# VectorE's order in a key phase, the load of the key weights, and the split of a routed update, in a linear-attention kernel with a routed MLP

## The chip, the core and the metric

The kernel runs on one core of one Trainium2 chip. The metric is the device time of one execution in microseconds; times before are the median of three runs. A profile is one further execution, taken by the hardware profiler; its span runs from the first to the last instruction.

The engines: PE (TensorE: matmuls and transposes through the array), PEld (the weight loads of PE), DVE (VectorE), ACT (ScalarE), POOL (GpSimd) and SP (SyncE, which here only issues DMAs). Each engine executes its own instructions in the order of the program and waits at semaphores for others.

## The reference

```
xn = layernorm(x)                              # x: 2048 x 640, no scale or bias
q, k, v = split(xn @ wqkv)                     # 32 heads of 20
phi = lambda t: where(t > 0, t + 1, exp(t)) + 1e-6
kv = einsum("bhsd,bhde", phi(k), v);  z = sum_s phi(k)
A  = ((phi(q) @ kv) / (phi(q) . z + 1e-6)) @ wo
r  = xn @ w_r                                  # a score of each row
idx = the 8 rows with the largest r
y  = ((silu(xn[idx] @ w_gate) * (xn[idx] @ w_up)) @ w_down) * sigmoid(r[idx])
B  = xn, with y added to the rows idx
out = x + A + B
```

All tensors are bfloat16.

## The kernel before

The 2048 rows are 16 tiles of 128 rows (t = 0 to 15), the 640 columns 5 blocks of 128 (kc). Tensors that stay in SBUF: `XX[:, t, 0, :]` holds the normalised tile and `XX[:, t, 1, :]` the input tile; `xnT` the normalised rows transposed; `pk` phi(k); `pqT` phi(q), transposed; `wk` the key weights. The values are never computed: `Gs`, the product of the normalised rows with phi(k), is multiplied by the value weights instead. All engines' instructions stand in an order written out by hand.

**Start (to about 19 us).** SP loads tiles 0, 1 and 2, then the key weights in two halves of 320 columns (`wkh[0]`, L112, and `wkh[1]`, L131), then tile 3 and the others. The second half lies in SBUF in rows of 321: its last column holds the router's vector `w_r`, which PE transposes into PSUM bank 3 (L128) and ACT copies (L130). Warm-up matmuls on zeros (L117, by `warm`) run on PE meanwhile. The first tiles are transposed by PE (`tr_pe`), tiles from 4 on by DMA transposes that SP issues (`tr_dma`, L205).

**The layer norm of a tile**, with the names of the program: `ln_a` and `ln_b` are the statistics of the left and the right half of the row on DVE (L148, L151), `ln_g` aggregates them (L154), `ln_s` adds epsilon on DVE (t of L173) and takes the square root as a power on POOL (s of L175), `ln_c` forms the centred tile c on ACT (L180) or DVE (L182), and `ln_xn` takes the reciprocal (L187) and scales c into `XX` (L189), both on DVE. For tiles 1 and 5 ACT makes the statistics (`ln_act`, `ln_var`).

**The k phase (about 19 to 54 us), a loop over t = 4 to 15 at L420.** `K(t)` is ten matmuls of the transposed tile by the key weights (L227, two halves into PSUM banks 6 and 7; the second half has the router's column too). `PHa(t)` takes Exp and Relu of both halves on ACT (L243, L246), `PHb(t)` forms phi(k) from them on DVE, min(exp, 1) + relu (L262, called the feature sum here), and `G(t)` accumulates nine matmuls into PSUM (L267, L272). PE's order is K(t), G(t-1). DVE's order in an iteration is: feature sum of t-1; reciprocal and scaling of tile t+2; both half statistics, the aggregate and t of tile t+3. ACT's is: four activations of tile t, then c of tile t+3. SP issues the transpose of tile t+2, and from t = 7 on a part of the query weights behind it; at t = 13 it issues the loads of the other weights (wv, wo, wg, wu).

**Residual.** x + xn is formed in place in `XX[:, t, 1, :]` (`xpx`): on DVE (L214) for tiles from `TF` on, at the end of the k phase, and on ACT (L217) for tiles below `TF`, during the output phase.

**The later phases (PE without a break from 47.6 us).** `q_pe` and `q_fin` make phi(q) in 20 blocks (L453, L508); between them stand the small products for kv, z and the routed MLP. From 87.5 us on `out_one(t)` multiplies by the merged output weights (L684), adds the residual on DVE (L698, for the last tile in two halves, L694) and stores the tile (SP; the second half of the last tile goes through ACT's queue).

**The routed update** is y for 8 rows. `TF` splits it: the residual tiles from TF on are written to a scratch in HBM (`hi_copy`), y is added there by an accumulating indirect DMA of POOL (`hi_add`, in `rows_add`, L712), and they are loaded back (`hi_load`) before their output tiles need them. For tiles below TF the outputs are stored first, and y is then added to the output in HBM by a second accumulating DMA (`fix_add`, the same line), which stands in front of the last output tile and waits for the stores of all tiles below TF. Rows outside of the half in question have an index out of bounds and are skipped.

Of the kernel before, what the change touches and what calls it, by code (L numbers as in the profile page):

```python
# [7 lines left out]
P = 128  # L8
S = 2048
D = 640  # L10
# [3 lines left out]
T = S // P  # L14
KC = D // P
# [7 lines left out]
FQ = F // 4  # L23
EPS_BF16 = 1.0013580322265625e-05
LOW = S - 1
TF = 12

BF16 = mybir.dt.bfloat16
F32 = mybir.dt.float32
# [7 lines left out]
def kernel(  # L37
# [13 lines left out]
    pe, dve, act, pool, sp = nc.tensor, nc.vector, nc.scalar, nc.gpsimd, nc.sync  # L51
# [3 lines left out]
    wqkv_v = A_wqkv.rearrange("(kc p) n -> p kc n", p=P)  # L55
# [7 lines left out]
    PS = psp.tile([P, 8, 512], F32, name="PS")  # L63

    def st(shape, dt, name, tag=None):
        return sb.tile(shape, dt, name=name, tag=tag or name)
# [2 lines left out]
    xnT = st([P, KC, S], BF16, "xnT")  # L69
    pk = st([P, T, D], BF16, "pk", "pkwd")  # L70
    pqT = st([P, KC, S], BF16, "pqT")
    wk = st([P, KC * (D + 1)], BF16, "wk", "wkM")
    wq = st([P, KC, D], BF16, "wq")
    wo1 = st([P, NG, D], BF16, "wo1")
    wo2 = st([P, D], BF16, "wo2")
# [5 lines left out]
    ident = st([P, P], BF16, "ident")  # L81
# [12 lines left out]
    MR = st([P, T], F32, "MR")  # L94

    HW = 320
    wkh = [wk[:, 0 : KC * HW].rearrange("p (k c) -> p k c", k=KC),
           wk[:, KC * HW : KC * (D + 1)].rearrange("p (k c) -> p k c", k=KC)]


    def ld(eng, dst, src):
        eng.dma_start(dst, src)
# [5 lines left out]
    wr = st([KC, P], BF16, "wr")  # L108
    ld(act, wr[:], B_w_r.rearrange("(kc p) -> kc p", p=P))
    ld(sp, XX[:, 1, 1, :], x_v[:, 1, :])  # L110
    ld(sp, XX[:, 2, 1, :], x_v[:, 2, :])
    ld(sp, wkh[0], wqkv_v[:, :, D : D + HW])  # L112


    def warm(n, w=512):
        for _ in range(n):
            pe.matmul(PS[:, 7, 0:w], lhsT=zero[:, 0:P], rhs=zero[:, 0:w], start=True, stop=True)  # L117
# [7 lines left out]
    dve.memset(ones32[:], 1.0)  # L125
    dve.memset(eps6[:], 1e-6)
    warm(4)
    pe.transpose(PS[:, 3, :].bitcast(BF16)[:, 0:KC], wr[:], ident[0:KC, 0:KC])  # L128
    warm(6)
    act.copy(wkh[1][:, :, HW], PS[:, 3, :].bitcast(BF16)[:, 0:KC])  # L130
    ld(sp, wkh[1][:, :, 0:HW], wqkv_v[:, :, D + HW : 2 * D])  # L131
    ld(sp, XX[:, 3, 1, :], x_v[:, 3, :])
    kv1 = st([P, NG, GC], BF16, "kv1")
    kv2 = st([P, NG, GC], BF16, "kv2")
# [11 lines left out]
    def ln_a(t):  # L146
        sts[t] = tmp.tile([P, 2, nc.vector.BN_STATS_DIM], F32, tag="stats", name="stats", bufs=3)
        dve.bn_stats(out=sts[t][:, 0, :], in_=XX[:, t, 1, 0:320])  # L148

    def ln_b(t):  # L150
        dve.bn_stats(out=sts[t][:, 1, :], in_=XX[:, t, 1, 320:D])  # L151

    def ln_g(t):
        dve.bn_aggr(out=MV[:, t, :], in_=sts[t][:])  # L154
# [15 lines left out]
    def ln_s(t, sg=1.0):  # L170
        t2 = tmp.tile([P, 1], BF16, tag="t2", name="t2", bufs=4)
        ss[t] = tmp.tile([P, 1], BF16, tag="s", name="s", bufs=4)
        dve.tensor_scalar(out=t2[:], in0=MV[:, t, 1:2], scalar1=sg, scalar2=EPS_BF16,  # L173
                          op0=ALU.mult, op1=ALU.add)
        pool.tensor_tensor(out=ss[t][:], in0=t2[:], in1=halfc[:], op=ALU.pow)  # L175

    def ln_c(t, eng):
        cs[t] = tmp.tile([P, D], BF16, tag="c", name="c", bufs=3)
        if eng is act:
            act.activation(cs[t][:], XX[:, t, 1, :], AF.Identity, bias=MVf[:, t, 0:1], scale=-1.0)  # L180
        else:
            dve.tensor_scalar(out=cs[t][:], in0=XX[:, t, 1, :], scalar1=MVf[:, t, 0:1], scalar2=-1.0,  # L182
                              op0=ALU.subtract, op1=ALU.mult)

    def ln_xn(t, parts=((0, D),)):
        c = cs[t]
        dve.reciprocal(SR[:, t : t + 1], ss[t][:])  # L187
        for a, b in parts:
            dve.tensor_scalar(out=XX[:, t, 0, a:b], in0=c[:, a:b], scalar1=SR[:, t : t + 1], scalar2=-1.0,  # L189
                              op0=ALU.mult, op1=ALU.mult)  # L190
# [13 lines left out]
    def tr_dma(t):  # L204
        sp.dma_start_transpose(xnT[:, :, t * P : (t + 1) * P], XX[:, t, 0, :])  # L205
# [6 lines left out]
    def xpx(t):  # L212
        if t >= TF:
            dve.tensor_scalar(out=XX[:, t, 1, :], in0=XX[:, t, 1, :], scalar1=SR1[:, t : t + 1],  # L214
                              scalar2=MR[:, t : t + 1], op0=ALU.mult, op1=ALU.add)
            return
        act.activation(XX[:, t, 1, :], XX[:, t, 1, :], AF.Identity, bias=MR[:, t : t + 1], scale=SR1[:, t : t + 1])  # L217


    def off(t, h):  # L220
        return T - 1 - t if t != 1 and h else 0

    def K(t, hs=(0, 1), b=6):
        for h in hs:
            w = HW + h
            for kc in range(KC):
                pe.matmul(  # L227
                    PS[:, b + h, off(t, h) : off(t, h) + w],
                    lhsT=xnT[:, kc, t * P : (t + 1) * P],
                    rhs=wkh[h][:, kc, 0:w],  # L230
                    start=(kc == 0),
                    stop=(kc == KC - 1),
                )
# [6 lines left out]
    def PHe(t, h, b=6):  # L240
        if h == 0:
            phis[t] = tuple(tmp.tile([P, D], BF16, tag=k, name=k, bufs=3) for k in ("ek", "rk"))
        act.activation(phis[t][0][:, h * HW : (h + 1) * HW], phi_src(t, h, b), AF.Exp)  # L243

    def PHr(t, h, b=6):
        act.activation(phis[t][1][:, h * HW : (h + 1) * HW], phi_src(t, h, b), AF.Relu)  # L246

    def PHa(t, hs=(0, 1), b=6):
        for h in hs:
            PHe(t, h, b)  # L250
            PHr(t, h, b)
# [8 lines left out]
    def PHb(t):  # L260
        ek, rk = phis[t]
        dve.scalar_tensor_tensor(out=pk[:, t, :], in0=ek[:], scalar=1.0, in1=rk[:], op0=ALU.min, op1=ALU.add)  # L262
# [99 lines left out]
    ln_xn(1)  # L362
    ln_g(2)
    ln_s(2)
    K(0, (0,))
    PHe(0, 0)
    tr_pe(1, 2, act, act)
    consts_e()
    bm2_copies(sp, (1, 2))
    PHr(0, 0)  # L370
    K(0, (1,))
    ln_c(2, dve)
    ln_a(3)
    ln_xn(2)
    PHa(0, (1,))
    K(1, (0,), 4)
    tr_pe(2, 0, act, act)
    K(1, (1,), 4)
# [16 lines left out]
    ln_s(4)  # L395
    PHr(2, 0)
    ln_c(4, dve)
    ln_xn(4)
    tr_dma(4)
    bm2_copies(act, (3,))  # L400
# [8 lines left out]
    ln_s(5, -1.0)  # L409
    ln_c(5, dve)  # L410
    PHa(3)
    ln_a(6)
    ln_xn(5)
    tr_dma(5)
    ln_b(6)
    ln_g(6)
    ln_s(6)
    ln_c(6, act)
# [1 line left out]
    for t in range(4, T):  # L420
        K(t)
        PHb(t - 1)
        if t + 2 < T:
            ln_xn(t + 2)
            tr_dma(t + 2)
        PHa(t)
        if t + 3 < T:
            ln_a(t + 3)
            ln_b(t + 3)
            ln_g(t + 3)  # L430
            ln_s(t + 3)
            ln_c(t + 3, act)
        if t == 13:
            xpx_cols(TF, T)
            xpx(TF)
        if t > 13:
            for i in range(2 if t == 14 else 1):
                xpx(TF + 1 + 2 * (t - 14) + i)
        G(t - 1)
        if t - 1 in pool_extra:  # L440
            pool_extra[t - 1]()
        if t > 4:
            loads(t)
# [261 lines left out]
    idxh = st([P, 1], I32, "idxh")  # L705
    hi_d = drp.tile([S - TF * P, D], BF16, name="hi_d")
    hi_4 = hi_d[:].rearrange("s (j c) -> (s j) c", j=4)
    hi_v = hi_d[:].rearrange("(t p) d -> p t d", p=P)
    out_lo = out[0][0 : TF * P, :].rearrange("s (j c) -> (s j) c", j=4)

# [175 lines left out]
```

## Time and profile before

| | us |
|---|---|
| median of three runs | 115.87 (115.63 to 115.9) |
| the profiled execution | 115.39 |
| its span, first to last instruction | 113.7 |

| engine | busy us | share of the span |
|---|---|---|
| PE | 105.9 | 93% |
| PEld | 65.0 | 57% |
| DVE | 83.8 | 74% |
| ACT | 76.2 | 67% |
| POOL | 24.2 | 21% |

The mean granted clock of PE is 0.994. DMAs move 18.72 MB, at 165 GB/s over the span. In a timeline a row gives the start, the duration, the engine, the line, the operation with its tiles and shapes, and in brackets the idle time of the engine just before with what ended it. Neighbouring instructions of one engine overlap a little in these records, so the distance of two starts says more than a duration. In the view of windows a row gives a stretch, its length, the busy time (and number of instructions) of PE, PEld, DVE, ACT and POOL, the granted clock, the busy share of the DMA engines and GB/s. A row of waits gives total time, number and longest one. A row of DMA issues gives KB each and the median time from issue to landing, where it is known.

### The profile page before, as it was taken

How to read it: one execution, taken by the hardware profiler on the slowest of the kernel's cores; microseconds unless marked ns; L12 is line 12 of the kernel's file. 1: busy time of each engine (PE TensorE's matmuls, PEld its weight loads, DVE VectorE, ACT ScalarE, POOL GpSimd, SP SyncE). 2: the span in 40 equal slices, each digit the busy share in tenths (PEclk: the TensorE clock that was granted, in tenths of full speed). 3: DMA queues.
4: the chain of work that ended last, by engine and by line, in shares of the span. 5: the costliest groups of instructions: out<-in, count | busy, mean ns of one | idle time of the engine just before them, and what ended most of it. 6: DMA issues, size and time to landing. Idle time of an engine off the chain costs nothing.

```text
span 113.7 us, 2754 instructions
## 1 busy us (share of the span) xinstructions
PE 105.9 (93%) x999; PEld 65.0 (57%) x999; DVE 83.8 (74%) x209; ACT 76.2 (67%) x168; POOL 24.2 (21%) x48
## 2 busy tenths in 40 slices
PE   5989997999899999999999999999999999999970
PEld 1356654665555555566657565656565767777740
DVE  1888898867777777784586996466867898869760
ACT  4649993866777766665199379799979965980000
POOL 7345214236433333300000002200033000000050
PEclk9999999999999999999999999999999999999997
DMA  3899932302344664429999946950712143693342
GB/s 87 244 271 356 310 64 53 62 21 39 61 115 115 63 159 89 99 58 279 355 390 401 403 145 167 389 160 26 244 42 47 35 141 118 123 378 131 127 157 62
DMA packets 22984, 18.72 MB, mean 165 GB/s; under 512 B 11194, under 2 KB 21690, under 8 KB 22970
## 3 DMA queue, kind: packets, MB, share of 16 engines
q1 hardware_dynamic: 22352, 18.36, 54.2%
q10 hardware_dynamic: 330, 0.16, 0.5%
q8 instruction: 8, 0.13, 0.5%
q0 software_dynamic: 288, 0.01, 0.3%
q14 instruction: 6, 0.05, 0.2%
HBM read 12.98 MB, written 3.49 MB: 145 GB/s over the span
## 4 chain that ended last, share of the span: by engine, by line
PE 50%; DVE 8%; POOL 3%; DMA 2%; POOLq 2%; issue 1%; ACT 0%; DVEq 0%
PE PS L453 19%; PE PS L684 14%; PE PS L267 4%; POOL s L175 3%; PE PS L227 2%; DMA out_dram<-o 2%; POOLq L881 2%; PE PS L622 2%; PE PS L628 2%; PE PS L646 1%; DVE stats L151 1%; DVE stats L148 1%; DVE XX L189 1%; PE PS L516 1%; PE PS L286 1%
## 5 line engine op out<-in xcount | busy, mean ns | idle before, releaser
L227 PE MATMUL PS<-wk,xnT 128*128 128x320 bf16 (+1 forms) x160 | 24.6, 300 | 1.0 <-DMA xnT<-XX 0.7
L267 PE MATMUL PS<-pk,XX 128*128 128x512 bf16 x80 | 23.2, 378 | 1.8 <-DVE pk L262 1.5
L453 PE MATMUL PS<-xnT,wq 128*128 128x512 bf16 x100 | 23.1, 380 | 0.0
L684 PE MATMUL PS<-Mb,pqT 128*128 128x320 bf16 x160 | 22.1, 299 | 0.0
L227 PEld LDWEIGHTS <-xnT 128*128 128x128 bf16 x160 | 15.3, 98 | 8.5 <-DMA xnT<-XX 1.3
L175 POOL TENSOR_TENSOR s<-t,halfc 128x1 bf16<-128x1 bf16 x16 | 14.0, 878 | 28.0 <-DVE t L173 28.0
L684 PEld LDWEIGHTS <-pqT 128*128 128x128 bf16 x160 | 15.5, 97 | 6.4
L453 PEld LDWEIGHTS <-wq 128*128 128x128 bf16 x100 | 11.4, 118 | 8.6
L243 ACT ACTIVATE ek<-PS 128x320 bf16<-128x320 f32 x32 | 14.0, 438 | 3.4 <-PE PS L227 3.3
L508 DVE SCALAR_TENSOR_TENSOR pqT<-qe,qr 128x512 bf16<-128x512 bf16 x20 | 13.5, 683 | 3.7 <-ACT qr L460 3.7
L459 ACT ACTIVATE qe<-PS 128x512 bf16<-128x512 f32 x20 | 12.1, 607 | 5.5 <-PE PS L453 5.4
L698 DVE TENSOR_TENSOR o<-PS,XX 128x640 bf16<-128x640 f32 x15 | 12.3, 823 | 3.9 <-PE PS L684 3.3
L180 ACT ACTIVATE c<-XX,MVf 128x640 bf16<-128x640 bf16 x10 | 8.3, 828 | 9.3 <-DVE MVf L154 5.5
L246 ACT ACTIVATE rk<-PS 128x320 bf16<-128x320 f32 x32 | 14.2, 443 | 0.0
L272 PE MATMUL PS<-pk,XX 128*128 128x128 bf16 x64 | 14.0, 218 | 0.0
L262 DVE SCALAR_TENSOR_TENSOR pk<-ek,rk 128x640 bf16<-128x640 bf16 x16 | 13.0, 817 | 0.6 <-ACT rk L246 0.6
L267 PEld LDWEIGHTS <-XX 128*128 128x128 bf16 x80 | 7.7, 97 | 8.1
L460 ACT ACTIVATE qr<-PS 128x512 bf16<-128x512 f32 x20 | 12.1, 607 | 0.0
L217 ACT ACTIVATE XX<-XX,MR,SR 128x640 bf16<-128x640 bf16 x12 | 10.2, 913 | 1.4 <-DVE o L698 1.4
L272 PEld LDWEIGHTS <-XX 128*128 128x128 bf16 x64 | 6.2, 97 | 4.3 <-issue 3.8
L148 DVE BATCH_NORM_STATS2 stats<-XX 128x6 f32<-128x320 bf16 x14 | 6.8, 488 | 2.5 <-DMA XX<-in_A_x_dram 2.4
L189 DVE TENSOR_SCALAR XX<-c,SR 128x640 bf16<-128x640 bf16 (+2 forms) x17 | 6.5, 387 | 1.7 <-ACT rk L246 0.5
(117 smaller groups left out, 100.5 us busy)
## 6 DMA issues: line engine op xcount, KB each, us to landing
out_dram<-o SPq DMA_DIRECT2D x15, 160.0 KB, 1.9
XX<-in_A_x_dram SPq DMA_DIRECT2D x6, 320.0 KB, 6.4
wg<-in_B_w_gate_dram SPq DMA_DIRECT2D x5, 384.0 KB, 6.8
wu<-in_B_w_up_dram SPq DMA_DIRECT2D x5, 384.0 KB, 6.9
wd<-in_B_w_down_dram SPq DMA_DIRECT2D x1, 1920.0 KB, 9.0
wk<-in_A_wqkv_dram SPq DMA_DIRECT2D x2, 400.0 KB, 4.3
wq<-in_A_wqkv_dram SPq DMA_DIRECT2D x5, 160.0 KB, 2.4
wv<-in_A_wqkv_dram SPq DMA_DIRECT2D x1, 800.0 KB, 4.8
```

Of the source, the lines that this page charges most:

```text
L175: pool.tensor_tensor(out=ss[t][:], in0=t2[:], in1=halfc[:], op=ALU.pow)
L227: pe.matmul(PS[:, b + h, off(t, h) : off(t, h) + w], lhsT=xnT[:, kc, t * P : (t + 1) * P], rhs=wkh[h][:, kc, 0:w], start=(kc == 0), stop=( ...
L243: act.activation(phis[t][0][:, h * HW : (h + 1) * HW], phi_src(t, h, b), AF.Exp)
L246: act.activation(phis[t][1][:, h * HW : (h + 1) * HW], phi_src(t, h, b), AF.Relu)
L262: dve.scalar_tensor_tensor(out=pk[:, t, :], in0=ek[:], scalar=1.0, in1=rk[:], op0=ALU.min, op1=ALU.add)
L267: pe.matmul(PS[:, a, :], lhsT=lhsT, rhs=pk[:, t, 0:512], start=(t == 0), stop=(t == T - 1),)
L272: pe.matmul(PS[:, 5, a * P : (a + 1) * P], lhsT=lhsT, rhs=pk[:, t, 512:D], start=(t == 0 and a == 0), stop=(t == T - 1), skip_group_check= ...
L453: pe.matmul(PS[:, bank, :], lhsT=by5(wq[:, kc, :])[:, m, :], rhs=xnT[:, kc, tb * TBLK : (tb + 1) * TBLK], start=(kc == 0), stop=(kc == KC ...
L459: act.activation(e, PS[:, bank, :], AF.Exp)
L508: dve.scalar_tensor_tensor(out=pqT[:, m, tb * TBLK : (tb + 1) * TBLK], in0=e, scalar=1.0, in1=r, op0=ALU.min, op1=ALU.add,)
L684: pe.matmul(PS[:, b + h, 0:HW], lhsT=pqT[:, kc, t * P : (t + 1) * P], rhs=Mb[:, kc, h * HW : (h + 1) * HW], start=(kc == 0), stop=(kc == K ...
L698: dve.tensor_tensor(out=ot[:].rearrange("p (h c) -> p h c", h=2), in0=PS[:, b : b + 2, 0:HW], in1=XX[:, t, 1, :].rearrange("p (h c) -> p h ...
```

## The change

Three edits in one.

1. In the k phase the first half statistic of a tile (`ln_a`) moves. For t below 9 it stands between the feature sum and the reciprocal of the same iteration; from t = 8 on the first half of tile t+4 is taken at the end of the iteration, ahead of the next feature sum (at t = 8 both happen). Ahead of the loop, the halves of tile 6 stand in front of `ln_xn(4)` and `ln_xn(5)`.
2. The key weights come in one load of whole rows of 640 columns; in SBUF the rows are 641 long, and both halves of K read from them. The router's column waits in PSUM bank 5 (before: 3), and ACT copies it behind the copies of the first transposed tile instead of ahead of the second load. There is one warm-up matmul less.
3. `TF` goes from 12 to 11: tile 11 passes from the group below TF to the group that goes through the scratch, its residual from ACT to DVE.

```diff
-TF = 12
+TF = 11
...
-    wk = st([P, KC * (D + 1)], BF16, "wk", "wkM")
+    wk = st([P, KC, D + 1], BF16, "wk", "wkM")
...
-    wkh = [wk[:, 0 : KC * HW].rearrange("p (k c) -> p k c", k=KC),
-           wk[:, KC * HW : KC * (D + 1)].rearrange("p (k c) -> p k c", k=KC)]
...
-    ld(sp, wkh[0], wqkv_v[:, :, D : D + HW])
+    ld(sp, wk[:, :, 0:D], wqkv_v[:, :, D : 2 * D])
...
     warm(4)
-    pe.transpose(PS[:, 3, :].bitcast(BF16)[:, 0:KC], wr[:], ident[0:KC, 0:KC])
-    warm(6)
-    act.copy(wkh[1][:, :, HW], PS[:, 3, :].bitcast(BF16)[:, 0:KC])
-    ld(sp, wkh[1][:, :, 0:HW], wqkv_v[:, :, D + HW : 2 * D])
+    pe.transpose(PS[:, 5, :].bitcast(BF16)[:, 0:KC], wr[:], ident[0:KC, 0:KC])
+    warm(5)
     ld(sp, XX[:, 3, 1, :], x_v[:, 3, :])
...
-                    rhs=wkh[h][:, kc, 0:w],
+                    rhs=wk[:, kc, h * HW : h * HW + w],
...
     ln_s(2)
+    act.copy(wk[:, :, D], PS[:, 5, :].bitcast(BF16)[:, 0:KC])
     K(0, (0,))
...
     ln_c(4, dve)
+    ln_a(6)
     ln_xn(4)
...
     PHa(3)
-    ln_a(6)
+    ln_b(6)
     ln_xn(5)
     tr_dma(5)
-    ln_b(6)
     ln_g(6)
...
         PHb(t - 1)
+        if t + 3 < T and t < 9:
+            ln_a(t + 3)
         if t + 2 < T:
             ln_xn(t + 2)
             tr_dma(t + 2)
         PHa(t)
         if t + 3 < T:
-            ln_a(t + 3)
             ln_b(t + 3)
             ln_g(t + 3)
             ln_s(t + 3)
             ln_c(t + 3, act)
+        if t + 4 < T and t >= 8:
+            ln_a(t + 4)
...
-            for i in range(2 if t == 14 else 1):
+            for i in range(2):
                 xpx(TF + 1 + 2 * (t - 14) + i)
```

## The prediction

> **What bounds the kernel now.** I read the page first: TensorE (PE) is busy 93% of the span, and the chain that ended last is PE from 47.6 us to 104.5 us with next to no gaps. Before that, from 35.7 to 46.9 us, the chain is something else, a loop through VectorE (DVE) and GpSimd (POOL), so I went to the k phase (the loop over t, about 19 to 54 us) and cut it at the starts of K(4) to K(15) in the view of windows. Three of the twelve:
>
> ```profile
> 21.74:24.42 2.68, 2.68 (x21) 1.69 (x19) 1.72 (x6) 2.24 (x5) 1.49 (x4) 1.00 0.32 64
> 36.70:39.88 3.18, 2.96 (x21) 1.64 (x19) 2.56 (x9) 2.14 (x5) 1.06 (x1) 1.00 0.56 58
> 48.94:51.62 2.68, 2.68 (x21) 1.69 (x20) 2.11 (x5) 1.43 (x4) 0.00 (x0) 1.00 0.49 76
> ```
>
> The first number is the length, then busy time of PE, its weight loads, DVE, ACT and POOL. A tile needs 2.68 us of PE; the tiles in the middle take about 3.06 to 3.18. Over 2.68 the nine intervals from K(6) at 24.42 to K(15) at 51.62 have 0.30, 0.49, 0.39, 0.38, 0.50, 0.26, 0.38, 0.38 and 0.00: **3.08 us** that PE doesn't need. The timeline of DVE for one such tile shows why:
>
> ```profile
> 37.59 0.81 DVE L262 SCALAR_TENSOR_TENSOR pk<-ek,rk 128x640 bf16<-128x640 bf16 x1
> 38.85 0.16 DVE L187 RECIPROCAL SR<-s 128x1 f32<-128x1 bf16 x1 [0.44 <-POOL s L175]
> 39.12 0.39 DVE L189 TENSOR_SCALAR XX<-c,SR 128x640 bf16<-128x640 bf16 x1
> 39.42 0.49 DVE L148 BATCH_NORM_STATS2 stats<-XX 128x6 f32<-128x320 bf16 x1
> 39.82 0.48 DVE L151 BATCH_NORM_STATS2 stats<-XX 128x6 f32<-128x320 bf16 x1
> 40.33 0.21 DVE L154 BATCH_NORM_AGGREGATE MVf<-stats 128x2 bf16<-128x12 f32 x1
> 40.58 0.16 DVE L173 TENSOR_SCALAR t<-MVf 128x1 bf16<-128x1 bf16 x1
> 40.65 0.82 DVE L262 SCALAR_TENSOR_TENSOR pk<-ek,rk 128x640 bf16<-128x640 bf16 x1
> ```
>
> From feature sum (L262) to feature sum 3.06 us pass, and 0.44 of them DVE waits for POOL's square root s (L175), which needs this tile's t. G(t) waits for the feature sum (six waits, 1.5 us on PE's view of waits), and the rest of the loss follows from it. In the view of waits this is 4.9 us in 11 waits of L187.
>
> How long POOL's power takes depends on what DVE runs beside it:
>
> ```profile
> 37.76 1.06 POOL L175 TENSOR_TENSOR s<-t,halfc 128x1 bf16<-128x1 bf16 x1 [2.00 <-DVE t L173]
> 16.70 0.62 POOL L175 TENSOR_TENSOR s<-t,halfc 128x1 bf16<-128x1 bf16 x1 [2.49 <-DVE t L173]
> 16.83 0.48 DVE L148 BATCH_NORM_STATS2 stats<-XX 128x6 f32<-128x320 bf16 x1
> ```
>
> At 37.76 it ends (38.82) 0.42 after the feature sum's end (38.40). At 16.70 it ends (17.32) 0.40 after the c of L182, which ran 16.54 to 16.92, while a half statistic runs from 16.83 to 17.31. So POOL seems held by the DVE instruction in front of it, then needs about 0.42, and a half statistic beside it doesn't hold it.
>
> **The k order, t below 9.** The first half statistic of tile t+3 goes from behind L189 into the gap behind the feature sum. Counts don't change, only places. New period from the rows: feature sum to reciprocal 38.85-37.59 = 1.26 (still set by POOL; 0.74 of sum plus 0.40 of statistic fit under it, 0.12 are left as wait), to L189 0.27, to the second statistic 0.30, to the aggregate 0.51, to t 0.25, to the next sum 0.07: 2.66 against 3.06. The whole 0.40 goes, and the loop is a hair below PE's 2.68. Then PE sets the pace and no more can be gained. L189, and with it the transpose that SP issues behind it, stands as far behind the sum as now, since the reciprocal waits for POOL in either order; ACT's c (L180) waits for the aggregate, which comes 0.40 earlier.
>
> **The order from t = 9 on.** The first half of tile t+4 stands behind t, ahead of the feature sum, so POOL's power (0.18 behind t) runs beside a statistic. Period: 0.07+0.40+0.74+0.27+0.30+0.51+0.25 = 2.54 if the power is out of the way, 2.69 if the sum waits until the power has had its 0.42 (0.18+0.42 = 0.60 behind t instead of 0.47, rounded up). Either is about PE's pace. What is given back: iteration 8 carries two first halves, 0.40 once; POOL's constants around 23 us held L189 from 23.29 to 23.70 and will again; one transpose took 2.18 us to issue (at 36.47), where 1.20 is usual. The sum may start 2.37 us (when ACT has finished) to 3.18 us (when G needs it, 4.05 less 0.87) behind its tile's K start, so 0.8 us of lag costs nothing and only what is above it stalls PE. All of the lags together are about 1.2 to 1.7, so I give back 0.5. Bounds: 3.08 (nothing given back) and 1.3 (rival one). Value: **2.6 us**. What follows is PE-bound, and its loads (wv, wo, wg, wu) are issued behind the last transposes, so all of it moves forward too.
>
> **Before the loop.** The first half of tile 6 takes the 0.44 us gap ahead of reciprocal 4, its second half the gap ahead of reciprocal 5 (17.35), so sum 3 comes 0.40 earlier than 18.69. No gain by itself: K(4) waits until 19.06 for a transpose, 0.68 us after PE's last busy record:
>
> ```profile
> 19.06 1.54 PE L227 MATMUL PS<-wk,xnT 128*128 128x320 bf16 x10 [0.68 <-DMA xnT<-XX]
> ```
>
> **The k weights in one load.** Now two of 400 KB, and the second waits for ACT's copy of the router column, though the columns differ:
>
> ```profile
> SPq L102 <- ACT wk L130: 0.9, 1, 0.9
> wk<-in_A_wqkv_dram SPq DMA_DIRECT2D x1, 400.0 KB, 4.3
> wv<-in_A_wqkv_dram SPq DMA_DIRECT2D x1, 800.0 KB, 4.8
> ```
>
> The first half was issued at 2.19 and landed 4.3 later, 6.49; K(0) began at 7.02, when xnT came. The whole is of wv's shape, which landed in 4.8 with nothing ahead; at 2.19 up to 1.3 us of x tiles are ahead (480 KB at some 350 GB/s, the rate of 9.5 to 10 us). So it lands at 7.0 to 8.3. The copy now stands on ACT behind the load and waits for it the same way (0.2 us with its hand-over), K(0) behind the copy; on ACT the first Exp and the copies of tile 1 are queued behind it. PE shifts by 0 to 1.3 us there, middle 0.6. Of this, 0.84 (18.22, where G(2) has been issued, to 19.06) is covered by the wait for the transpose; past it up to 0.5 shows. Against it: SP no longer stands from 2.62 to 3.49, so the x tile of L148's wait at 8.73 (0.57 us) may come up to 0.57 earlier and with it the transpose of tile 4, worth at most 0.4. I take **0.0**, bounds 0.4 gained to 0.5 lost. One warm-up matmul less (0.43) leaves PE idle from about 5.54 to 5.78: nothing waits for it.
>
> **Eleven tiles by accumulating DMA.** ACT loses one L217 (0.91 us, late, where it has 8 us free after 101.8); DVE gains one L214 (0.44) at t = 15, where it has no statistics left: free. hi_copy and hi_load grow from 640 to 800 KB, some 0.5 us each at 355 GB/s; the POOL add behind hi_copy started at 84.30 and its result is fetched at 96.57, so nine us cover it, and SP's stores queued behind hi_load have seven o buffers. At the end POOL's add waits for the store of tile 10 instead of 11, issued 1.46 us earlier (104.23 against 105.69). But two waits end together there:
>
> ```profile
> L881 SPq EVENT_SEMAPHORE  x2: 17/1030/2042, 110.4 to 110.4; - x2
> L881 POOLq DRAIN  x1: 3344/3344/3344, 109.0 to 109.0; - x1
> ```
>
> POOL's drain ends at 112.34, SP's wait for the last store at 112.44. Without POOL's part the store still ends there. I take **0.1** (fewer packets beside it), bounds 0 and 0.3.
>
> **Sum.** 2.6 + 0.0 + 0.1 = 2.7 us, against the profiled execution's own 115.39 (span 113.7 and 1.7 around it): 112.7. That execution is 0.48 below the median of the runs, 115.87, so the forecast for the median is **113.2 us**; its own range from the bounds is 112.2 to 114.0.
>
> **The rivals.**
> One: the wait is only partly removed, because POOL's power now gets ahead of the feature sum and holds it, or the transposes, issued 5.06 us behind a K start and needed 8.04 behind it, land late. For: the power's start, 0.18 behind t, is ahead of the sum wherever a statistic or ACT delays the sum. Against: only 0.42 of its time seems its own. If the sum is held by 0.35 in each tile the period is 2.89, and of 3.08 some 1.3 remain: 114.5 us.
> The Trainium skill's page "SBUF — State Buffer", section "Who interferes with whom", says that a DVE instruction with two SBUF inputs and a GpSimd instruction that reads SBUF lock each other out, whichever is first, for the whole instruction. The 1.06 against 0.62 us here agrees; by that rule the 0.35 is sure from t = 9 on and the time would lie between the two.
> Two: no change. If a statistic holds POOL as the sum does, the power ends 0.42 behind it, and the reciprocal stands at 0.74+0.40+0.42 = 1.56 with 0.07 of hand-over: 3.0 again, 115.7 us. The record at 16.70 speaks against it.
> Three, slower: the clock. With one warm-up matmul less and 0.24 us idle before the first transposes, PE could stay at its half rate (a 128x512 warm-up takes 0.43 apart at first, 0.22 later) through the early K and G. PE work from 6 to 18 us is 11 us; at half rate for all of it, 11 - 0.84 - 2.7 = 7.5 lost, 123 us; it decides against the change once the half rate lasts over 3.5 us of such work. Against: 0.68 us of idle before K(4) left the pace of its ten matmuls (1.54 us) as it is in every later K.
> The page "TensorE: Matmul & The Clock Gate", Part 1 of the Trainium skill, has the clock change after a window of about 3.4 us, so one missed window would cost an estimated 1.7 us, no sign change.
>
> **Chances.** Forecast 0.62, partial 0.20, no change 0.08, slower 0.10 (the clock, or what I don't see). 0.3% (0.35 us) is about what a measurement of this kernel can tell from none. Faster 0.82, same 0.08, slower 0.10. The range, 112.2 to 115.2, takes in most of the partial case.
>
> **What would show it.** DVE's reciprocal waits fall from 0.44 to about 0.1, K starts lie 2.68 to 2.75 apart from K(6) on, and DVE's loop leaves the chain. K(4) stays at 18.6 to 19.5. The last two waits: POOL's drain ends about 1.4 before SP's. I am wrong if K starts still lie 3.0 apart, if the sum waits behind the power, or if K(0) starts after 8.5 and K(4) moves with it.

## The result, and the profile after

| | us |
|---|---|
| before, median of 4 runs beside it | 115.89 (115.63 to 116.25) |
| after, median of 4 runs | 112.82 (111.42 to 114.36) |
| after / before | 0.9642, interval 0.9575 to 0.9709 |
| the profiled execution of after | 113.53 |
| its span | 111.7 (before: 113.7) |

The changed kernel is faster. Its executions fall into two groups by the mean granted clock of PE, and the ratio is made from the two in which the clock was kept (111.42 and 112.11); it stands for 0.9642 * 115.89 = 111.7 us. The forecast was 113.2, with 112.2 as its low end: the direction is right, and the gain of those executions is larger than I allowed.

The profiled execution is one of the others, so it shows what the change gains and what it loses in one picture. First the three intervals between K starts that answer to those of before, in the view of windows (length, busy time of PE, its weight loads, DVE, ACT and POOL, clock, DMA share, GB/s):

```profile
22.48:25.22 2.74, 2.74 (x21) 1.65 (x20) 2.52 (x8) 2.15 (x5) 1.61 (x4) 1.00 0.56 63
36.10:39.55 3.45, 2.83 (x20) 1.63 (x19) 3.27 (x10) 3.03 (x6) 1.10 (x2) 1.00 1.01 79
47.56:50.23 2.67, 2.67 (x20) 1.68 (x19) 1.54 (x4) 1.43 (x4) 0.00 (x0) 1.00 0.75 171
```

In ten of the eleven intervals from K(4) at 19.81 to K(15) at 50.23 PE is now busy from end to end, 2.66 to 2.84 us each. One, in front of K(11), is 3.45 and holds a wait of 0.62. K(4) to K(15) takes 30.42, against 32.56 before. DVE's timeline shows the new order, with no idle time in front of the reciprocal (L183, before L187):

```profile
28.20 0.81 DVE L258 SCALAR_TENSOR_TENSOR pk<-ek,rk 128x640 bf16<-128x640 bf16 x1
28.93 0.49 DVE L144 BATCH_NORM_STATS2 stats<-XX 128x6 f32<-128x320 bf16 x1
29.46 0.17 DVE L183 RECIPROCAL SR<-s 128x1 f32<-128x1 bf16 x1
29.73 0.39 DVE L185 TENSOR_SCALAR XX<-c,SR 128x640 bf16<-128x640 bf16 x1
30.03 0.48 DVE L147 BATCH_NORM_STATS2 stats<-XX 128x6 f32<-128x320 bf16 x1
30.55 0.21 DVE L150 BATCH_NORM_AGGREGATE MVf<-stats 128x2 bf16<-128x12 f32 x1
30.80 0.16 DVE L169 TENSOR_SCALAR t<-MVf 128x1 bf16<-128x1 bf16 x1
30.87 0.82 DVE L258 SCALAR_TENSOR_TENSOR pk<-ek,rk 128x640 bf16<-128x640 bf16 x1
```

From sum to sum 2.67 us, where 3.06 passed before. Ahead of the loop, PE's timeline has the loss. K(0) starts at 7.95 (before 7.02), after 1.39 us of waiting for the key weights, and its five matmuls and the next ten are slow (2.50 for ten, 1.53 later):

```profile
7.95 1.33 PE L223 MATMUL PS<-wk,xnT 128*128 128x320 bf16 x5 [1.39 <-DMA wk<-in_A_wqkv_dram]
9.06 0.74 PE L192 MATMUL PS<-ident,XX 128*128 128x128 bf16 x5
9.60 2.50 PE L223 MATMUL PS<-wk,xnT 128*128 128x321 bf16 x10
```

The view of windows says why: the granted clock (third number from the end) is at half, from about 8.2 to 11.6.

```profile
8.00:8.50 0.50, 0.50 (x3) 0.29 (x3) 0.34 (x2) 0.11 (x1) 0.47 (x1) 0.66 1.05 387
8.50:9.00 0.50, 0.50 (x3) 0.30 (x2) 0.47 (x3) 0.00 (x0) 0.43 (x3) 0.50 1.07 389
11.00:11.50 0.50, 0.50 (x4) 0.27 (x3) 0.45 (x2) 0.32 (x1) 0.00 (x0) 0.50 1.09 371
11.50:12.00 0.50, 0.50 (x6) 0.38 (x5) 0.12 (x2) 0.45 (x2) 0.00 (x0) 0.93 1.05 353
```

At the end, L881's rows (duration in ns: shortest, median, longest; then first and last start in us) show no wait of SP like the 2042 ns of before, and POOL's drain starts at 105.2, not 109.0 (the last store is still waited for; what the tail consists of stands with the experiments):

```profile
L881 SPq EVENT_SEMAPHORE  x9: 17/28/28, 109.0 to 111.7; - x9
L881 POOLq DRAIN  x3: 40/107/3330, 105.2 to 111.4; - x3
```

From PE's last matmul to the end of the span 3.1 us pass, where it was 3.7. From K(15) to PE's end it is 58.36 to 58.38 in every profile of this study but that of `warm_more`. So every span can be written as a ledger of four terms: the start of K(4); K(4) to K(15); 58.37; the tail, behind PE's last matmul.

| us | K(4) | K(4) to K(15) | to PE's end | tail | span |
|---|---|---|---|---|---|
| before | 19.06 | 32.56 | 58.37 | 3.69 | 113.7 |
| after, profiled | 19.81 | 30.42 | 58.36 | 3.12 | 111.7 |

The change has won 2.14 in the k phase and 0.57 in the tail, and has lost 0.75 ahead of K(4).

### The profile page after: what moved, and what is told of

Same layout as the page of the kernel before. It is cut to its first block, busy times and chain, and to the rows that moved or that the text cites. A ratio compares the mean times of both kernels' runs of the same rounds, so it can differ in the third digit from the quotient of the medians.

```text
span 111.7 us, 2749 instructions
## 1 busy us (share of the span) xinstructions
PE 104.8 (94%) x998; PEld 65.2 (58%) x998; DVE 84.3 (75%) x210; ACT 75.8 (68%) x167; POOL 21.7 (19%) x48
## 4 chain that ended last, share of the span: by engine, by line
PE 66%; DVE 9%; DMA 9%; ACT 5%; POOL 4%; issue 2%; SPq 1%; ACTq 1%; DVEq 0%; POOLq 0%
PE PS L684 20%; PE PS L453 20%; PE PS L223 10%; PE PS L263 6%; DMA wk<-in_A_wqkv_dram 5%; POOL s L171 4%; DMA xnT<-XX 4%; DVE XX L185 3%; DVE stats L147 2%; ACT ek L239 2%; PE PS L622 2%; PE PS L628 2%; PE PS L646 1%; ACT rk L242 1%; PE PS L268 1%
## 5 line engine op out<-in xcount | busy, mean ns | idle before, releaser
L223 PE MATMUL PS<-wk,xnT 128*128 128x320 bf16 (+1 forms) x160 | 25.9, 311 | 2.0 <-DMA wk<-in_A_wqkv_dram 1.4
L171 POOL TENSOR_TENSOR s<-t,halfc 128x1 bf16<-128x1 bf16 x16 | 11.7, 733 | 27.1 <-DVE t L169 27.1
L263 PEld LDWEIGHTS <-XX 128*128 128x128 bf16 x80 | 7.7, 98 | 8.1
L213 ACT ACTIVATE XX<-XX,MR,SR 128x640 bf16<-128x640 bf16 x11 | 9.4, 914 | 1.7 <-issue 1.7
L144 DVE BATCH_NORM_STATS2 stats<-XX 128x6 f32<-128x320 bf16 x14 | 6.8, 488 | 2.2 <-DMA XX<-in_A_x_dram 2.2
L147 DVE BATCH_NORM_STATS2 stats<-XX 128x6 f32<-128x320 bf16 x14 | 6.8, 484 | 0.0
```

The costliest lines, as they stand in the source:

```text
L223: pe.matmul(PS[:, b + h, off(t, h) : off(t, h) + w], lhsT=xnT[:, kc, t * P : (t + 1) * P], rhs=wk[:, kc, h * HW : h * HW + w], start=(kc = ...
L263: pe.matmul(PS[:, a, :], lhsT=lhsT, rhs=pk[:, t, 0:512], start=(t == 0), stop=(t == T - 1),)
```

## The experiments

My theory going in: the order on DVE is the whole gain, the load of whole rows lengthens the start by PE's wait and by the clock, and `TF` is worth a few tenths. The rival: the load brings something as well, because SP no longer stands behind ACT's copy, and the order alone brings less than 2.6.

**Each part alone, and the change again.** `again` is the changed kernel itself; `order_only`, `tf_only` and `wk_only` are before with one of the three edits.

> The changed kernel once more. Theory A (the change as three separate gains, and a clock that is sometimes lost at the start): executions fall into two groups, near 111.4 to 112.1 us where TensorE keeps its clock while it waits about 1.4 us for the key weights, and near 113.5 to 114.4 us where it runs at half rate for one stretch of about 3.5 us. With the clock kept, K(4) starts before 19.0 us, K(15) about 49.0 to 49.5 us (before: 51.62), and the stretch from TensorE's last matmul to the end is 3.1 us (before: 3.7). Rival B (one gain, all of it in the k phase): K(15) starts at 47.6 us and the end stretch is 3.7 us.

> The kernel before with the new places of the half statistics alone. Theory A: the K starts from K(6) to K(15) close up to about 2.7 us, with one late transpose left: 2.1 to 2.9 us faster, 113.0 to 113.8 us, with little scatter, since the start is as before. Rival B: all of the gain, 4 us, 111.9 us. Rival C (the start is what gained): at most 1 us.

> The kernel before with the load of whole rows (copy of the router column behind it, one warm-up matmul less) alone. Theory A: K(0) waits until 7.9 us for the weights, 0.9 us later than before; K(4) waits for a transpose anyway, so the time is within 0.5 us of before where the clock is kept, and 0.5 to 2 us slower where it is lost for one stretch. Rival C (the load is a gain because tile 3 comes earlier): 0.5 to 1 us faster.

> The kernel before with eleven tiles instead of twelve by the accumulating DMA. Theory A: the accumulation ends before the last store begins, the last store takes about 0.5 us less, and the time falls by 0.5 to 0.6 us. The forecast on record (the last store ends the kernel anyway): 0 to 0.3 us.

| | median us | ratio to before (interval) | K(4) | K(4) to K(15) | tail |
|---|---|---|---|---|---|
| order_only | 113.28 (112.9 to 113.92) | 0.9784 (0.9754 to 0.9813) | 19.12 | 29.85 | 4.14 |
| wk_only | 118.03 (115.77 to 119.87) | 1.0062 (1.0024 to 1.0101) | 20.46 | 33.70 | 3.99 |
| tf_only | 115.63 (115.1 to 115.97) | 0.9975 (0.9959 to 0.9991) | 19.15 | 32.51 | 3.42 |
| again | 114.84 (112.49 to 116.16) | | 21.17 | 30.35 | 3.13 |

`again` came out otherwise than expected: its one execution with the clock kept and a short time took 112.49 us, another with the clock kept took 115.31, and the profiled one waited 2.71 us for the key weights and lost the clock.

The order alone takes 32.56 to 29.85: 2.71 us, where I had said 2.6. Its windows, K(4), K(10) and K(11):

```profile
19.12:21.79 2.67, 2.61 (x18) 1.70 (x20) 1.85 (x7) 1.78 (x5) 0.91 (x4) 1.00 0.54 103
35.18:38.26 3.08, 2.78 (x19) 1.63 (x19) 2.90 (x9) 2.59 (x6) 0.92 (x2) 1.00 1.03 93
38.26:40.93 2.67, 2.67 (x19) 1.70 (x20) 2.20 (x8) 1.72 (x5) 0.55 (x1) 1.00 0.74 168
```

Every interval is 2.67 but the one in front of K(11), which is 0.41 longer. That one wait is all that separates 2.71 from 3.12. The load of whole rows by itself costs time. Its ratio is made from the five shortest of 12 executions; in eight of the 12 the clock was lost (0.966 to 0.985), and those took 117.5 to 119.9 us, more than I had expected. PE's timeline in its profiled execution, and two of its windows:

```profile
8.90 1.49 PE L223 MATMUL PS<-wk,xnT 128*128 128x320 bf16 x5 [1.56 <-DMA wk<-in_A_wqkv_dram]
```

```profile
9.00:10.00 1.00, 1.00 (x5) 0.53 (x5) 0.66 (x4) 0.06 (x1) 0.93 (x3) 0.50 1.07 373
10.00:11.00 1.00, 1.00 (x9) 0.76 (x8) 0.93 (x4) 0.58 (x2) 0.46 (x2) 0.50 1.07 369
```

So the rival falls: by itself the load costs. In its profile K(4) comes 1.40 later than in before's, and the k phase behind it takes 1.14 longer. The product of the parts that don't touch the load is 0.9784 * 0.9975 = 0.976.

The load does bring something in a place where neither theory looked, the tail. At the end SP goes through a list of waits, one entry after the other, for its own queues and those of other engines. Counted from PE's last matmul, the last store lands at 2.46 us in before and at 2.19 in `tf_only` and `after`. This 0.27 is what `TF` gives: the accumulation is done by then. In every kernel with the two half loads the last store's semaphore stands near the head of the list, and five waits follow it; from its landing to SP's drain 0.37 pass in before and in `tf_only`. In every kernel with the load of whole rows it stands last, and 0.08 pass in `after`. That is the other 0.30 of the tail's 0.57, and it comes with the second edit. Without `TF` the tail also depends on when the accumulation lands: in `order_only` that is 2.98 behind PE's last matmul, later than the store.

**The two good parts together, and the start mended in two ways.** `order_tf` has the order and `TF` but the old loads. `warm_more` is the changed kernel with PE kept busy until the weights land. `halves_free` is `order_tf` with both half loads back to back (the router's column copied later, from bank 5), so that K(0) needs 400 KB and not 800.

```diff
# warm_more, against after (one line, behind the transposes of tile 0)
-    warm(1)
+    warm(10)
# halves_free, against order_tf
     ld(sp, wkh[0], wqkv_v[:, :, D : D + HW])
+    ld(sp, wkh[1][:, :, 0:HW], wqkv_v[:, :, D + HW : 2 * D])
...
-    act.copy(wkh[1][:, :, HW], PS[:, 3, :].bitcast(BF16)[:, 0:KC])
-    ld(sp, wkh[1][:, :, 0:HW], wqkv_v[:, :, D + HW : 2 * D])
...
     PHe(0, 0)
+    act.copy(wkh[1][:, :, HW], PS[:, 5, :].bitcast(BF16)[:, 0:KC])
```

> The change without its load of whole rows (order and eleven tiles alone, two half loads as before). If the parts add up, 2.5 us from the order and 0.3 from the tiles: 112.9 to 113.3 us, with a scatter of 1 us at most. If the load of whole rows is needed for the 111.4 us that single executions of the changed kernel reach (theory A: it brings the transpose of tile 4 out of the way while the clock is kept), no execution here is under 112.2. If it is no part of it (rival: chance in the k phase), some are.

> The changed kernel with ten warm-up matmuls instead of one behind the first transposes, so that TensorE is busy until about 8.4 us while it waits for the key weights. Theory A (its slow executions are those in which the clock falls to half for one stretch of 3.4 us while TensorE idles): the granted clock stays at 1.00, the executions gather at 111.2 to 112.3 us, and K(4) starts at 18.0 to 18.9 us. Rival (the late landing of the weights itself costs the time): median still above 113.5 us.

> Order and eleven tiles, with two half loads issued back to back; the router column is copied behind the first Exp, so that no load waits for a copy and the first half of K(0) waits for the first load alone. Theory A (what the load of whole rows gives is that SP doesn't stand behind a copy, and what it costs is that K(0) waits for all of the weights): K(0) starts at 7.0 to 7.3 us as before, the clock is kept, K(4) starts before 18.9, and the time is 111.6 to 112.6 us with little scatter. Rival (whole rows are what gains): as order_tf, 113 us.

| | median us | ratio to before (interval) | K(0) | K(4) | K(4) to K(15) | tail |
|---|---|---|---|---|---|---|
| order_tf | 112.9 (112.64 to 113.64) | 0.974 (0.9705 to 0.9776) | 7.07 | 19.54 | 29.83 | 3.42 |
| warm_more | 113.13 (112.31 to 113.92) | 0.9741 (0.969 to 0.9793) | 8.32 | 19.37 | 29.36 | 3.38 |
| halves_free | 112.5 (112.14 to 112.56) | 0.969 (0.9661 to 0.972) | 7.12 | 19.02 | 29.91 | 3.4 |

With PE busy the clock stays at 1.00 in the profiled execution and between 0.994 and 1.0 in the six timed ones, although K(0) comes at 8.32, later than in the first profile of after. Its time still scatters: three executions lie at 112.3 to 112.65 and three at 113.6 to 113.9, and both its time and its K(4) lie above what I had expected. The profiled one, of the upper group, has a wait of 1.23 us at 69 us, for small transfers of the phase of z that took 3.0 to 3.8 us; what the lower group did there no profile shows. In `halves_free`, with K(0) needing half the bytes, PE's waits are short and the times of six executions lie within 0.42 us.

But one thing didn't fit: in all of these K(4) starts between 19.0 and 19.6 behind a wait, however early or late K(0) was. I had taken this wait, in the prediction, for the transpose's own landing time.

**The wait in front of K(4).** The traces hold two queues named "instruction". The packets of one, q8, are 16 KB each, some 20 us apart early on and closer together later, and PE issues most instructions here. Set beside K(4):

```
                 transpose issued   packet            K(4)    K(4) - its end   PE's wait
before                14.86         16.99 to 17.91    19.06       1.15           0.68
order_only            14.84         16.97 to 17.98    19.12       1.14           0.76
halves_free           14.71         16.94 to 17.87    19.02       1.15           0.78
again3                14.66         17.21 to 18.13    19.28       1.15           1.09
warm_four             14.62         17.17 to 18.09    19.24       1.15           0.75
warm_more             14.85         17.31 to 18.23    19.37       1.14           0.54
order_tf              15.23         17.47 to 18.39    19.54       1.15           0.78
```

K(4) follows the end of the packet by 1.14 or 1.15 us in all seven, while its distance from the transpose's issue runs from 4.2 to 4.6. The packets of the transpose itself show how. It moves 640 packets of 256 bytes and ends with 32 of 4 bytes. In `order_tf` 30 of these 32 start between 17.12 and 17.35, and the last two at 18.38 and 18.39, when the instruction packet ends. Of its 16 landings, 15 stand at 17.70 to 17.87 and the last at 19.49, 0.05 in front of K(4). In the other six the last two of the 32 likewise start within 0.02 of the instruction packet's end. So one of the sixteen parts of the transpose stood behind the packet.

The transposes in front of K(11) have the same: with a packet in flight beside them they took 3.3 to 4.5 us to their last landing, otherwise mostly 2.6. So has the wait of 1.23 us in `warm_more`: of the 16 landings of its last small transfer 15 stand by 66.40 and the last at 68.49, 1.20 behind the end of an instruction packet (66.36 to 67.29). To test it I moved the packet: the ten warm-ups of 512 columns became twenty of 256 columns, the same PE time but ten more matmuls and ten more weight loads, so that the later instructions stand further back in PE's program. `order_tf_pad8` does it to the first four alone, and `before_pad` does it to the kernel before.

```diff
# order_tf_pad against order_tf, before_pad against before
-    warm(4)
+    warm(8, 256)
...
-    warm(6)
+    warm(12, 256)
```

> As order_tf, with the same warm-up time cut into twice as many matmuls of half the width (20 more TensorE instructions ahead of everything). Theory D (the transposes that land in 3.4 to 4.2 us instead of 2.6 are those during which the instruction queue of TensorE fetches its next 16 KB, near 16 and near 36 us): the fetches come about 1.4 us earlier, K(4) waits less than the 0.7 us of before or another transpose is hit, and the time moves by 0.3 to 1 us. Rival (the first transpose is slow by itself): K(4) at 19.1 us and the time of order_tf, within 0.2 us.

> The kernel before, its warm-up time cut into twice as many matmuls of half the width (20 more TensorE instructions ahead of everything, nothing else changed). Theory D (K(4) can't start until 2.1 to 2.2 us after TensorE's instruction fetch, since the last part of the transpose of tile 4 stands behind it): the fetch comes near 15.6 instead of 16.9 us, K(4) starts at 18.2 to 18.4 instead of 19.06, where TensorE has finished G(2); the time falls by at most 0.8 us, and by less if the loop behind it is held by VectorE. Rival (the first DMA transpose is slow by itself): K(4) at 19.1, same time.

> As order_tf with 8 more TensorE instructions ahead instead of 20. Theory D: the fetch comes about 0.5 us earlier than in order_tf, K(4) stands 2.1 to 2.2 us behind it (about 19.0 us if the fetch is at 16.9), and the time lies between order_tf (112.9) and order_tf_pad (111.8): 112.2 to 112.6 us. Rival (any change of the warm-ups gives the whole 1 us): 111.8 us.

| | median us | ratio to before (interval) | packet | K(4) | its wait |
|---|---|---|---|---|---|
| order_tf_pad | 111.84 (111.5 to 111.96) | 0.9634 (0.9605 to 0.9664) | 15.78 to 17.02 | 18.67 | none on PE |
| order_tf_pad8 | 112.47 (112.17 to 113.15) | 0.9706 (0.9671 to 0.9741) | 17.26 to 18.25 | 19.39 | 0.85 |
| before_pad | 115.97 (115.41 to 117.49) | 1.000 (0.9968 to 1.0031) | 16.03 to 17.43 | 19.05 | none on PE |

In `order_tf_pad` the transpose of tile 4 is issued at 15.23, to the hundredth as in `order_tf`. The packet comes 1.7 us earlier, and K(4), K(5) and, further on, K(11) show no wait on PE:

```profile
18.67 1.54 PE L227 MATMUL PS<-wk,xnT 128*128 128x320 bf16 x10
21.35 1.53 PE L227 MATMUL PS<-wk,xnT 128*128 128x320 bf16 x10
...
37.40 1.53 PE L227 MATMUL PS<-wk,xnT 128*128 128x320 bf16 x10
```

That is 1.06 us for ten narrow pairs of warm-ups; between the two profiles it is 0.98, of which K(4) has 0.87 and K(11) 0.40, less 0.29 in the tail, where the accumulation came late. The wait is shorter, but not gone: K(4) still starts 0.05 behind the transpose's last landing (18.62), and the load of its weights waits for that:

```profile
18.66 1.21 PEld L227 LDWEIGHTS <-xnT 128*128 128x128 bf16 x10 [0.24 <-DMA xnT<-XX]
```

The packet now runs beside the first data of the transpose, and 19 packets of these take up to 0.92 us instead of 0.05. From issue to last landing 3.4 us pass, where it was 4.3.

`order_tf_pad8` moves the packet by 0.2 only; it still holds the last part of the transpose, and K(4) follows its end by 1.14. Its profile is 0.15 shorter than that of `order_tf`; the times are lower by 0.4, and the rest isn't explained.

On the kernel before, K(4) comes no sooner (19.05) and the time doesn't change, which I had thought it might. The second half of the key weights held K(0) for 0.88 there (0.18 in before's profile), and the transpose is issued 0.54 later (15.40). It lands at 19.00, 0.05 in front of K(4), and the load of K(4)'s weights waits 0.45 for it. So `before_pad` doesn't tell what the packet is worth in that kernel.

**Both mends at once.** `best` is `halves_free` with the narrow warm-ups.

> Order, eleven tiles, the two half loads back to back without the copy between, and the narrow warm-ups. If what the free load gives (0.4 us, 112.5 against 112.9) and what the place of the fetch gives (1.1 us, 111.8 against 112.9) add: 111.2 to 111.5 us. If both remove the same wait: 111.8 us.

111.39 us (111.14 to 111.92), ratio 0.9621 (0.9588 to 0.9655). K(0) and K(4) of its profiled execution:

```profile
6.88 0.85 PE L226 MATMUL PS<-wk,xnT 128*128 128x320 bf16 x5 [0.21 <-ACT xnT L199]
...
18.27 1.54 PE L226 MATMUL PS<-wk,xnT 128*128 128x320 bf16 x10
```

Its six executions lie within 0.8 us, where the changed kernel's lie up to 4.7 apart (111.42 to 116.16). It beats the kernel before. Against the changed kernel the intervals of the two ratios overlap, but only one of that kernel's 22 executions (111.42) is shorter than the longest of `best` (111.92).

**The changed kernel again, and a shorter cover.** What was left open is why the changed kernel comes out at 111.4 at one time and 116 at another. `again2`, `again3` and `again4` are the changed kernel; `warm_four` has `warm(4)` in place of the `warm(1)` behind the transposes of tile 0.

> The changed kernel for one more profile. If it is an execution with the clock kept: K(0) starts at 7.5 to 8.5 us, the matmuls behind it keep full pace, K(4) starts at 18.4 to 19.3 us, either where TensorE has finished G(2) or 2.1 to 2.2 us behind the instruction fetch, and the stretch from TensorE's last matmul to the end is 3.1 us. If the clock falls: ten matmuls of K take 2.5 us near 10 us.

> The changed kernel with four warm-up matmuls instead of one behind the first transposes: TensorE idles for at most some 0.7 us before K(0), with 6 instructions more ahead of the fetch instead of the 18 of warm_more. Theory A with D: where the clock is kept, the fetch falls near 17.6 to 18.2 us, behind the transpose of tile 4, K(4) starts where TensorE has finished G(2), at 18.4 to 19.0 us, and the time is 111.3 to 112.3 us. Rival (the changed start gives nothing even with the clock kept): K(4) at 19.1 us or later, 112.4 to 112.9 us.

> The changed kernel, for a profile of an execution that keeps its clock. If there is one: K(0) at 7.5 to 8.5 us, the fetch behind 17.6 us, K(4) at 18.4 to 19.0 us with no wait for the transpose, K(15) at 48 to 49 us.

> The changed kernel, a second try for a profile of an execution that keeps its clock, with the same numbers: K(4) at 18.4 to 19.0 us and K(15) at 48 to 49 us if it does; K(4) at 19.6 us or later if the clock falls near 9 us.

| | time of the profiled execution | clock | wait for wk | K(0) | K(4) | K(4) to K(15) | tail | span |
|---|---|---|---|---|---|---|---|---|
| again3 | 112.66 | 1.000 | 0.43 | 7.57 | 19.28 | 30.17 | 3.1 | 110.9 |
| again2 | 112.98 | 0.982 | 0.96 | 7.79 | 19.66 | 30.11 | 3.1 | 111.3 |
| after | 113.53 | 0.985 | 1.39 | 7.95 | 19.81 | 30.42 | 3.1 | 111.7 |
| again | 114.83 | 0.980 | 2.71 | 9.30 | 21.17 | 30.35 | 3.1 | 113.0 |
| again4 | 115.61 | 0.970 | 2.82 | 9.37 | 22.28 | 30.11 | 3.1 | 113.9 |
| warm_four | 111.81 | 0.999 | 0 | 7.98 | 19.24 | 29.35 | 3.1 | 110.1 |

The five executions of the one kernel differ in when its key weights land and in what follows from that at K(4); K(4) to K(15) differs by 0.3, the tail by 0.01. Issued at 2.19, they landed at 7.91 in the first profile and at about 9.3 in two others. It is the last few of the load's 16 parts that scatter: in all five profiles 12 of them or more had landed by 7.3. A wait of 0.43 in front of K(0) left the clock alone; waits of 0.96 and more came with a stretch at half rate, of 3.4 us in `after`, `again2` and `again` and of 6.8 in `again4` (8.1 to 15.0). It isn't that one wait alone. Adding up PE's idle time from 5.2 us to the second half of K(0), the profiles that lost the clock have 1.7 us (`again2`) to 3.4 us (`again4`), and those that kept it at most 1.3 us (`order_tf_pad`). Here are K(0), K(4) and K(11) of `again3`:

```profile
7.57 0.84 PE L223 MATMUL PS<-wk,xnT 128*128 128x320 bf16 x5 [0.43 <-DMA wk<-in_A_wqkv_dram]
...
19.28 1.54 PE L223 MATMUL PS<-wk,xnT 128*128 128x320 bf16 x10 [1.09 <-DMA xnT<-XX]
...
38.77 1.54 PE L223 MATMUL PS<-wk,xnT 128*128 128x320 bf16 x10 [0.65 <-DMA xnT<-XX]
```

`warm_four` starts K(0) at 7.98, as late as the first profile of after (7.95). The difference in front of it is that PE was busy. K(0) takes 0.84 instead of 1.33, and K(4) comes at 19.24 instead of 19.81:

```profile
7.98 0.84 PE L223 MATMUL PS<-wk,xnT 128*128 128x320 bf16 x5
...
19.24 1.54 PE L223 MATMUL PS<-wk,xnT 128*128 128x320 bf16 x10 [0.75 <-DMA xnT<-XX]
```

Its median over six is 111.92 (111.77 to 114.08), ratio 0.9647 (0.9618 to 0.9675); one of the six, 114.08, lost the clock all the same (0.983). The time is what I had expected of it, but not for the reason given: the packet came at 17.17 and K(4) at 19.24, where the rival had it. Against `order_tf` its span is 1.08 shorter: 0.30 at K(4), 0.48 for the wait at K(11) that it doesn't have, and 0.30 in the tail.

Over 22 executions of the changed kernel, from `after` to `again4`, the clock was kept (0.997 and above) in 7, which took 111.42 to 112.66 and once 115.31, and lost (0.985 and below) in 15, which took 112.98 to 116.16. In the later sets the ratio was 0.9743 (0.9696 to 0.979, `again3`; 0.9698 to 0.9788, `again4`), 112.9 on the same scale, and these sets take in executions of 113.5 to 113.8 that had lost the clock. `again3` was to show K(4) at 18.4 to 19.0 with no wait; it has 19.28 and a wait of 1.09. Two things stay open: why the last part of the load lands at 7.5 in one execution and at 9.3 in another, and what the execution of 111.42 looked like inside, since none of that speed was profiled.

## Why the prediction was right, and where it was wrong

The direction and the bound were right; the time, 111.7, lies below the range. What failed are sizes: the 0.5 given back in the k phase, the 0.1 for the tail, the 0.48 added for the median, and, in the executions that lost the clock, the 0.0 for the start.

**The bound was read rightly.** The k phase hung on the loop from t over POOL's power to the reciprocal. With the statistic between, the loop takes 2.67 for the 2.66 worked out (t below 9), and 2.53 and 2.52 at t = 9 and 10 for the 2.54 to 2.69. The reciprocal's 4.9 us in 11 waits are gone from the view of waits altogether.

**The first step that failed is the size of what the k order gives back:** "All of the lags together are about 1.2 to 1.7, so I give back 0.5". The lags on DVE cost nothing: with all twelve starts 2.67 apart K(4) to K(15) takes 29.35 (`warm_four`), 3.21 less than before and beyond my bound of 3.08. What the other kernels with the new order give back is, in the main, the wait in front of K(11), 0.4 to 0.8 of that interval, which goes with the instruction packet and not with DVE. In four profiles of the changed kernel the interval in front of K(8) is 0.2 longer too, and K(8) starts 0.05 behind the last landing of its transpose. So the term is 3.1 to 3.2 without such waits and 2.1 to 2.7 with them, where I had 2.6.

**The second is the tail,** "I take 0.1 (fewer packets beside it), bounds 0 and 0.3", and its reason, "Without POOL's part the store still ends there". The tail is 3.12 or 3.13 in all five profiles of the changed kernel, against 3.69 in before's: 0.57. `tf_only` gives 0.29 by its times (0.0025 * 115.9) and tails of 3.42 against 3.69 in the traces. The packets of the last store ran from 110.0 to 110.4 with no other queue's beside them, where before they ran from 111.5 to 112.1, beside those of the accumulation to 111.9. So this part, the one that I meant, is 0.27, near my upper bound. The other 0.30 is the place of the last wait in SP's list, which comes with the load of whole rows, and which the sum doesn't have.

**The third is the start,** "I take 0.0, bounds 0.4 gained to 0.5 lost". K(0) was to move by 0 to 1.3; it moved by 0.55 to 2.35. I let PE's idle time there cost its own length alone. In `after` K(4) lost 0.75, in `again` 2.1 and in `again4` 3.2, through the wait and the half clock that follows it. It is the third rival, "the clock", on a smaller scale: a stretch of 3.4 us or, in `again4`, of 6.8, and not of 11; and another idle time brings it, the one in front of K(0) and not the one ahead of the first transposes. K(0) to K(3) took 7.89 us in `after` and 6.38 in `again3`, so the shorter stretch costs 1.5 us of PE's time, of which the wait in front of K(4) covers up to 1.09 (that of `again3`). The Trainium skill's page "TensorE: Matmul & The Clock Gate", Part 1, has one window of about 3.4 us, from which the prediction estimated 1.7: the stretch in `after` agrees, and that in `again4` is about two of them. Its warning is for idle gaps of more than that window, and here one of 1.39, with 0.56 of idle time shortly before it, was enough.

**The cover was named wrongly.** I counted 0.84 of slack in front of K(4) as a wait for a transpose. It is a wait for a transpose that an instruction packet holds back; with the packet 1.7 us earlier, the same transpose was there 0.87 us sooner. So the slack isn't a property of the transposes, and it can be had as gain.

**The ledger of the miss.** 113.2 less 111.7 is 1.5. In the execution of `warm_four`, which ran at 111.81, the k order gives 3.21 for 2.6, the tail 0.57 for 0.1, and K(4) is 0.18 late for 0.0: 3.6 for 2.7. The rest is the step from the profiled execution to the median: I added the 0.48 by which before's profiled execution lay below its median, and the quick executions of after don't carry it. That these are the very terms in the execution of 111.42 is argued, not shown. The profiled execution of `again3`, the changed kernel itself with its clock kept, has 2.39 in the k phase, 0.57 in the tail and K(4) 0.22 late: 2.74, which is the sum forecast, by errors that cancel. How far the result lies below the range is chance in part: it rests on two executions, 111.42 and 112.11, and the other five that kept the clock took 112.27 to 112.66 and once 115.31. In the sets where the ratio was 0.974 the gains are partly paid back at K(4) and K(11), and the time lands near 113.

**Rivals one and two fell.** The sum is not held by POOL's power from t = 9 on. POOL and DVE in the timeline of after:

```profile
38.83 0.55 POOL L171 TENSOR_TENSOR s<-t,halfc 128x1 bf16<-128x1 bf16 x1 [2.04 <-DVE t L169]
...
38.52 0.16 DVE L169 TENSOR_SCALAR t<-MVf 128x1 bf16<-128x1 bf16 x1
38.59 0.48 DVE L144 BATCH_NORM_STATS2 stats<-XX 128x6 f32<-128x320 bf16 x1
38.99 0.81 DVE L258 SCALAR_TENSOR_TENSOR pk<-ek,rk 128x640 bf16<-128x640 bf16 x1
```

The power takes 0.55 beside the statistic, where it took 1.05 beside a sum (at 31.04 in the same trace); so the statistic doesn't hold POOL (rival two). The sum starts at 38.99, 0.40 behind the statistic as everywhere, while the power still runs, and keeps its 0.81 (rival one). The Trainium skill's page "SBUF — State Buffer", section "Who interferes with whom", would have the sum wait for the power, since it came second; this trace agrees for the power beside the sum, and doesn't for the sum behind the power.

## What to carry to other kernels

A wait on a short round trip over another engine is best filled with independent work of the engine that waits: the gain is the whole wait until the next engine's pace is met (3.08 us worked out from the gaps, 3.21 in `warm_four`). A load ahead of the first matmuls is to be priced by the spread of its landing and by what PE's clock does after the idle time, not by its mean; cut it into the piece that the first matmul needs, or keep PE busy until it lands. And where a wait is put down to a DMA, see what else its queues carried at that moment before counting it as fixed slack.

## What was not expected of the hardware

PE's instruction stream comes in by DMA packets of 16 KB (8 on the page, 0.13 MB), and a transpose in flight beside one lands late: where PE waits in front of K(4), K(4) starts 1.14 or 1.15 us behind the packet's end, since the last of the transpose's 16 parts stands behind the packet. Ten more matmuls and their weight loads ahead of it moved the packet by 1.7 us and were worth 1.06 us (112.9 to 111.84). That the packets are PE's is inferred: they move with the number of PE's instructions. That the two share one DMA engine is likely from this, but the traces don't name the engine of a packet.

An idle PE of 1 to 1.4 us in front of K(0), some 7 us into the kernel, brought 3.4 us at half the clock, one of 2.71 no more than that, one of 2.82 (with 0.58 shortly before) 6.8, and 0.43 us did not.

The order in which SP waits for its queues at the end of the kernel is worth 0.30 us: 0.37 pass from the last store's landing to SP's drain where five waits follow it, 0.08 where none does.
